# Issuing one stage's stores from GpSimd's queue instead of SyncE's

## The chip, the core and the metric

The kernel runs on one core of one Trainium2 chip. The metric is the device time of one execution in microseconds, as the median of several runs. A profile of one execution goes with it. The engines are named as in the profile: PE (TensorE's matmuls; PEld its weight loads), DVE (VectorE), ACT (ScalarE), POOL (GpSimd) and SP (SyncE). "SPq" is SP's queue of instructions that issue DMAs.

## The reference

The inputs are q, k and v of shape (4, 8, 576, 64) and two pairs of weights, (512, 2048) and (2048, 512). Three stages follow each other:

```python
# attention inside chunks of 64 rows
scores = q_c @ k_c.T / sqrt(64); attn = softmax(scores); out = attn @ v_c
x = out as (2304, 512)
# layer 1: mish
h = x @ w_in;  g = h * tanh(softplus(h));  x = g @ w_out
# layer 2: squareplus
h = x @ w_in2; g = h if h >= 1, 0 if h <= -1, else (h + 1)**2 / 4;  out = g @ w_out2
```

Everything is float32. The kernel reaches that accuracy by splitting each operand into a high and a low part and adding three matmuls for each product (high x high, high x low, low x high).

## The kernel before

**The stages.** The 2304 tokens are cut into 18 tiles of 128. Tiles 0 to 5 go through attention first. Layer 1's first product then has two forms. For the first 768 tokens (two blocks b of 384) it is plain: `up(b, j)` (L672) makes product j of 16 for a block with 12 matmuls (L687) into a bank of PSUM ring "B", 32 products in all. Meanwhile PE runs the attention of tiles 6 to 17 (transposes L558, scores L574, transposes L618, values L630), whose results are the tokens of the second form: `up_seven` (L911), a Strassen-like scheme with seven products (L934) for the other 1536 tokens. The second product of layer 1 is L737, layer 2 is L998 and L811.

**The z buffers.** After `up(b, j)`, ACT applies Mish (L1070) from PSUM into a tile z of the ring "z0", which has three buffers, and one DMA stores the tile to device memory (`spill[j]`, L1073; 192 KB for 384 columns). Much later `g_load` (L715) reads it back for the second product. So a Mish may start only when the store of the Mish three before has landed. ACT takes its instructions in order, so what stands behind the Mish waits too.

**Weights.** `w_part` (L330) loads a block of w_in (L350), decodes it (ACT L358, DVE L365), and splits it: a high part `hi` (L319 on ACT or L321 on DVE) and a low part `lo` (L375), which goes to POOL or DVE. POOL's other work in this stage is the normalisation of attention (L609).

**The order of the work.** `Plan` (L26) keeps a list of all operations with the engine (or the engines to choose from), a planned duration, what they read and write, and a priority. `order()` (L75) simulates the engines with these durations and writes down the order; each engine then runs its instructions in just that order (L1168 to L1184). A DMA is an operation of SP of 0.65 us, then a transfer in a common DMA stream and a lag of 2.2 us until it counts as landed (L141 to L143). All DMAs of this kernel are issued by SP, loads and stores alike, in one planned order. Waits are made from the dependencies; an instruction whose wait is not over holds up all that stand behind it on its engine.

Of the kernel before, what the change touches and what calls it, by code (L numbers as in the profile page):

```python
# [166 lines left out]
def kernel(  # L167
# [20 lines left out]
    nc = tc.nc  # L188
# [97 lines left out]
    def new(name, tag, shape, dtype=F32):  # L286
        size = 4
        for d in shape[1:]:
            size *= d
        at = PLACES[name[0]](*name[1:]) if tag is None else None  # L290
        plan.tile(name, tag, at, size)
        specs[name] = (tag, shape, dtype, size)

    def get(name):
        if name not in T:
            tag, shape, dtype, size = specs[name]
            tile = plan.tiles[name]
            if tag in PSUM:
                t = banks[tag][tile["slot"]]
            elif tag in LENT:  # L300
                at = LENT[tag][2] + tile["slot"] * LENT[tag][1]
                t = area(at, size, F32)
            elif tag is None:
                a, n = WITHIN.get(name[:2], lambda _: (tile["at"], size))(name[-1])
                t = area(a, n)[:, (tile["at"] - a) // 4:(tile["at"] + size - a) // 4]
            else:
                at = base[tag] + tile["slot"] * FIXED[tag][1]
                t = memory[:, at // 4:(at + size) // 4]
                if dtype == U32:
                    t = t.bitcast(dtype)  # L310
            if len(shape) > 2:
                dims = " ".join("abcd"[:len(shape) - 1])
                t = t.rearrange(f"p ({dims}) -> p {dims}", **dict(zip("abcd", shape[1:])))
            T[name] = t
        return T[name]
# [7 lines left out]
    def op(engine, length, emit, **kw):  # L323
        return plan.op(engine, length, emit, **kw)

    def dma(kb, emit, **kw):
        op("SP", 0.65, emit, size=kb * kw.pop("slow", 0.83) / 300.0, **kw)


    def w_part(n, j, tau, release=0.0, after=(), pair=None):  # L330
# [45 lines left out]

        kw = {"prio": tau, "release": release}
        dma(512, load, slow=(1.05, 0.83)[n % 2], reads=after, writes=[raw], tiles=[raw], **kw)
        kw = {"prio": tau}

# [4 lines left out]
        if n == 2:  # L385
            dma(256, lambda _: nc.sync.dma_start(out=wd[j // 2][:, j % 2 * DM:(j % 2 + 1) * DM], in_=get(sh)),
                reads=[sh], writes=[("wd", n, j)], tiles=[sh], prio=tau)
            return
# [6 lines left out]
    def w_load(n, jp, tau, release=0.0, after=()):  # L395
        wf = ("wf", n, jp)
        new(wf, "ld", [P, 2, DM])
        dma(512, lambda _: nc.sync.dma_start(out=get(wf).rearrange("p j f -> p (j f)"), in_=wd[jp]),
            reads=[("wd", n, 2 * jp), ("wd", n, 2 * jp + 1), *after], writes=[wf], tiles=[wf], prio=tau, release=release)
        return wf  # L400
# [271 lines left out]
    def up(b, j, tau):  # L672
        h, w = ("h", 0, b, j), ("w", 0, j)
        new(h, "B", [P, 512])
        start, width = PART(b, j)
        tiles = range(start // P, (start + width) // P)
        x = ("x", OF[tiles[-1]])

        def products(some):
            wt = get(w)  # L680
            xt = get(x).rearrange("p i r k t -> p r k i t")
            xt = xt[:, :, :, tiles[0] - FIRST[x[1]] // P:tiles[-1] + 1 - FIRST[x[1]] // P]
            ps = get(h)[:, 0:width].rearrange("p (i t) -> p i t", t=P)
            for kk in some:
                wh, wl = wt[:, 0, kk * P:(kk + 1) * P], wt[:, 1, kk * P:(kk + 1) * P]
                for y, (a, r) in enumerate(((wh, 0), (wh, 1), (wl, 0))):
                    nc.tensor.matmul(  # L687
                        out=ps, lhsT=a, rhs=xt[:, r, kk],
                        start=(kk == 0 and y == 0), stop=(kk == KD - 1 and y == 2),
                    )  # L690

        n = PIECES if b == 0 and j < EACH else 1
        for k in range(n):
            op("PE", long(width) / n, lambda _, k=k: products(range(k * KD // n, (k + 1) * KD // n)),
               reads=[(x, y, i, c) for y in range(2) for c in range(2) for i in tiles] + [(w, 0), (w, 1)],
               writes=[h], tiles=[h, w, x], prio=tau, late=LATE if n > 1 and k == 0 else 0.0)
        return h, start, width
# [366 lines left out]
    for b in range(len(UP)):  # L1064
        for j in range(NF):
            tau = due(b, j)
            h, start, width = up(b, j, tau)
            z = ("z", 0, b, j)
            new(z, "z0", [P, width])
            op("ACT", 0.17 + width / 1220, lambda _, h=h, z=z, width=width: nc.scalar.activation(  # L1070
                out=get(z), in_=get(h)[:, 0:width], func=AF.Mish
            ), reads=[h], writes=[z], tiles=[h, z], table="mish", prio=tau)
            dma(width / 2, lambda _, z=z, j=j, start=start, width=width: nc.sync.dma_start(  # L1073
                out=spill[j][:, start:start + width], in_=get(z)
            ), reads=[z], writes=[("spill", 0, b, j)], tiles=[z], prio=tau)
    units1 = [(jp, q) for some in (range(NF // 4, NF // 2), range(NF // 4)) for q in (1, 2) for jp in some]
# [138 lines left out]
```

## Time and profile before

| | |
|---|---|
| Time, median of 3 runs | 821.62 us (820.94 to 822.12) |
| Profiled execution, its time | 822.98 us |
| its span, first to last instruction | 821.1 us |
| PE busy in the span | 806.0 us (98%) |
| DVE, ACT, POOL busy | 615.7, 468.7, 43.5 us |
| DMA queues | one for the program's DMAs, 166,736 packets, 212.33 MB |

The profile's page lists the busy time of each engine and the costliest groups of instructions; the trace behind it answers for a stretch, a line or an engine. Times in rows are from the start of the span. In a timeline a row may merge several instructions (xN); what stands in square brackets is the idle time of the engine before the row and what ended it. Matmuls overlap, so rows of PE can overlap by part of a microsecond. The span is 1.9 us shorter than the time of the same execution.

### The profile page before, as it was taken

Reading aid. Unit: us, or ns where it says so; the run is one execution under the profiler, and the core shown is the slowest. Engines: PE = TensorE matmul, PEld = TensorE weight load, DVE = VectorE, ACT = ScalarE, POOL = GpSimd, SP = SyncE. Lnnn points to the kernel's source line nnn. Section 1 sums busy time; section 2 is a strip of 40 time slices with the busy share of each in tenths; the row PEclk is TensorE's granted clock in tenths of the full one; section 3 lists DMA queues with packets and bytes.
Section 4 is the critical chain, followed back from the end, with each engine's and each line's share of the span. In section 5 each row is a group of like instructions: output and inputs, shape, how many; then the busy total and the mean of one; then the engine's idle time right before and its main releaser. Section 6 shows DMA issues by size and latency. Waiting matters only on the chain.

```text
span 821.1 us, 15929 instructions
## 1 busy us (share of the span) xinstructions
PE 806.0 (98%) x6002; PEld 762.7 (93%) x6002; DVE 615.7 (75%) x1092; ACT 468.7 (57%) x733; POOL 43.5 (5%) x39
## 2 busy tenths in 40 slices
PE   8999989999999999999999999999999999999998
PEld 7888979999999988888888899999999999999998
DVE  4876658988888776766777879766777678888883
ACT  4778769756777654545465566655665543333341
POOL 2122111100013000000000000000000000000000
PEclk9999999999999999999999999999999999999999
DMA  9988773479899999899999694796669954444431
GB/s 208 235 247 225 191 178 101 155 249 321 278 367 368 370 386 406 345 395 377 380 407 377 197 345 139 241 367 198 230 254 407 415 184 152 144 139 129 130 103 52
DMA packets 166812, 213.33 MB, mean 260 GB/s; under 512 B 65232, under 2 KB 134352, under 8 KB 163664
## 3 DMA queue, kind: packets, MB, share of 16 engines
q1 hardware_dynamic: 166736, 212.33, 76.3%
q8 instruction: 47, 0.77, 0.4%
q14 instruction: 29, 0.24, 0.1%
HBM read 131.55 MB, written 80.74 MB: 259 GB/s over the span
## 4 chain that ended last, share of the span: by engine, by line
PE 91%; DMA 4%; SPq 2%; DVE 1%; ACT 0%; issue 0%; POOL 0%; ACTq 0%; POOLq 0%; DVEq 0%
PE A L737 13%; PE A L811 11%; PE B L811 11%; PE A L998 11%; PE B L998 11%; PE B L737 11%; PE B L934 9%; PE B L687 5%; PE A L934 4%; DMA memory<-in_moe_w_in_dram 2%; PE A L558 2%; DMA memory<-in_q_dram 1%; SPq L547 1%; PE A L630 1%; PE A L618 1%; PE A L574 1%
## 5 line engine op out<-in xcount | busy, mean ns | idle before, releaser
L319 ACT ACTIVATE r<-memory 128x512 fp32r<-128x512 f32 (+3 forms) x235 | 160.6, 710 | 155.6 <-DVE memory L769 28.2
L737 PE MATMUL A<-r,r 128*128 128x512 f32 (+1 forms) x576 | 114.2, 354 | 0.0
L737 PEld LDWEIGHTS A<-r,r 128*128 128x128 f32 x576 | 95.7, 189 | 14.8
L811 PE MATMUL A<-r,r 128*128 128x256 f32 x768 | 95.9, 283 | 0.0
L811 PEld LDWEIGHTS A<-r,r 128*128 128x128 f32 x768 | 93.9, 192 | 0.0
L811 PE MATMUL B<-r,r 128*128 128x256 f32 x744 | 93.0, 283 | 0.0
L998 PE MATMUL B<-r,r 128*128 128x384 f32 x504 | 92.6, 335 | 0.0
L998 PE MATMUL A<-r,r 128*128 128x384 f32 x504 | 91.1, 334 | 0.0
L811 PEld LDWEIGHTS B<-r,r 128*128 128x128 f32 x744 | 90.9, 192 | 0.0
L737 PE MATMUL B<-r,r 128*128 128x512 f32 x384 | 89.2, 389 | 0.0
L998 PEld LDWEIGHTS B<-r,r 128*128 128x128 f32 x504 | 88.1, 188 | 0.7
L998 PEld LDWEIGHTS A<-r,r 128*128 128x128 f32 x504 | 87.6, 188 | 0.4 <-ACT memory L319 0.3
L737 PEld LDWEIGHTS B<-r,r 128*128 128x128 f32 x384 | 71.9, 188 | 14.8
L783 DVE TENSOR_TENSOR r<-memory,r 128x768 fp32r<-128x768 f32 (+1 forms) x72 | 76.7, 1088 | 11.2 <-ACT r L319 11.1
L934 PE MATMUL B<-r,r 128*128 128x384 f32 x462 | 83.2, 336 | 0.0
L934 PEld LDWEIGHTS B<-r,r 128*128 128x128 f32 x462 | 79.9, 188 | 0.2
L687 PE MATMUL B<-r,r 128*128 128x384 f32 (+2 forms) x384 | 75.6, 345 | 1.5 <-POOL r L375 0.7
L358 ACT ACTIVATE memory<-memory 128x512 f16<-128x512 bf16 x72 | 55.9, 787 | 30.0 <-DMA memory<-in_moe_w_in_dram 15.1
L687 PEld LDWEIGHTS B<-r,r 128*128 128x128 f32 x384 | 65.0, 189 | 4.0 <-POOL r L375 1.2
L720 DVE TENSOR_TENSOR r<-memory,r 128x512 fp32r<-128x512 f32 (+1 forms) x80 | 49.6, 636 | 20.8 <-ACT r L319 20.8
L365 DVE SCALAR_TENSOR_TENSOR memory<-memory 128x512 uint32<-128x512 uint32 x72 | 50.7, 711 | 16.7 <-ACT memory L358 16.6
L769 DVE TENSOR_TENSOR memory<-memory 128x256 f32<-128x256 f32 (+1 forms) x108 | 53.4, 511 | 12.5 <-DMA memory<-z 11.2
(78 smaller groups left out, 954.8 us busy)
## 6 DMA issues: line engine op xcount, KB each, us to landing
memory<-z SPq DMA_DIRECT2D x136, 256.0 KB, 5.2
z<-memory SPq DMA_DIRECT2D x64, 384.0 KB, 4.9
memory<-in_moe_w_in_dram SPq DMA_DIRECT2D x40, 511.0 KB, 5.9
v<-r SPq DMA_DIRECT2D x16, 1024.0 KB, 8.3
memory<-in_moe_w_out_dram SPq DMA_DIRECT2D x32, 511.8 KB, 6.7
v<-r SPq DMA_DIRECT2D x16, 768.0 KB, 7.0
r<-v SPq DMA_DIRECT2D x20, 512.0 KB, 5.5
r<-v SPq DMA_DIRECT2D x8, 1024.0 KB, 10.6
```

The lines of the kernel that those rows point to most:

```text
L319: nc.scalar.activation(out=out, in_=in_, func=AF.Copy)
L358: nc.scalar.activation(out=get(dec).bitcast(F16).rearrange("p (f w) -> p f w", w=2)[:, :, 1], in_=get(raw).rearrange("p f w -> p (f w)").b ...
L365: nc.vector.scalar_tensor_tensor(out=to(sh).bitcast(U32), in0=get(raw)[:, :, 0], scalar=13, in1=get(dec).bitcast(U32), op0=ALU.logical_shi ...
L558: nc.tensor.transpose(out=get(ps)[:, p, :], in_=get(qk)[:, x, 2 * p:2 * p + 2, :].rearrange("t h d -> t (h d)"), identity=ident,)
L687: nc.tensor.matmul(out=ps, lhsT=a, rhs=xt[:, r, kk], start=(kk == 0 and y == 0), stop=(kk == KD - 1 and y == 2),)
L720: op("DVE", 0.15 + width / 930, port=True, emit=lambda _: nc.vector.tensor_tensor(out=get(g)[:, 1], in0=get(zl), in1=get(g)[:, 0].bitcast( ...
L737: nc.tensor.matmul(out=get(y)[:, 0:width], lhsT=l, rhs=r, start=(j == 0 and x == 0), stop=(j == NF - 1 and x == 2))
L769: op("DVE", length, lambda _: nc.vector.tensor_tensor(out=out(), in0=a(), in1=b(), op=ALU.subtract), port=True, reads=reads, writes=writes ...
L783: op("DVE", length, lambda _, a=a, b=b, x=x, c=c: nc.vector.tensor_tensor(out=get(g)[:, :, 1, a:b], in0=get(x)[:, :, c:], in1=get(g)[:, :, ...
L811: nc.tensor.matmul(out=get(ys[bank(x)])[:, half], lhsT=gt[:, l, c], rhs=wt[:, a, r], start=(j == 0 and (half == 0 or end) and y == 0), sto ...
L934: nc.tensor.matmul(out=ps, lhsT=l, rhs=xt[:, r, kk, :], start=(first and kk == 0 and y == 0), stop=(kk == 1 and y == 2), skip_group_check= ...
L998: nc.tensor.matmul(out=ps, lhsT=l, rhs=xt[:, r, kk, :], start=(first and kk == 0 and y == 0), stop=(kk == 1 and y == 2), skip_group_check= ...
```

## The change

The helper `dma` takes an engine and a planned duration, SP and 0.65 us unless something else is given. The store of z after the plain first product of layer 1 gives POOL and 1.1 us, and its DMA is issued with `nc.gpsimd.dma_start`. These are 32 DMAs. Data, sizes, buffers and priorities stay the same; the planner works out a new order for all engines from the new entry.

```diff
     def dma(kb, emit, **kw):
-        op("SP", 0.65, emit, size=kb * kw.pop("slow", 0.83) / 300.0, **kw)
+        at, length = kw.pop("by", ("SP", 0.65))
+        op(at, length, emit, size=kb * kw.pop("slow", 0.83) / 300.0, **kw)
...
-            dma(width / 2, lambda _, z=z, j=j, start=start, width=width: nc.sync.dma_start(
+            dma(width / 2, by=("POOL", 1.1), emit=lambda _, z=z, j=j, start=start, width=width: nc.gpsimd.dma_start(
                 out=spill[j][:, start:start + width], in_=get(z)
             ), reads=[z], writes=[("spill", 0, b, j)], tiles=[z], prio=tau)
```

## Rows read from the trace of the kernel before

**Rows 1.** The profile's page, part 1: busy us of each engine, share of the span.

```profile
PE 806.0 (98%) x6002; PEld 762.7 (93%) x6002; DVE 615.7 (75%) x1092; ACT 468.7 (57%) x733; POOL 43.5 (5%) x39
```

**Rows 2.** Stretches: length; PE, PEld, DVE, ACT, POOL busy us (instructions); clock, DMA share, GB/s.

```profile
30.00:100.00 70.00, 66.57 (x826) 60.42 (x815) 49.48 (x109) 55.27 (x85) 17.35 (x14) 1.00 0.87 227
100.00:110.00 10.00, 6.60 (x119) 5.84 (x118) 5.57 (x11) 3.53 (x7) 0.00 (x0) 0.92 0.86 214
110.00:160.00 50.00, 49.75 (x637) 46.26 (x637) 41.63 (x87) 42.52 (x65) 9.35 (x7) 0.98 0.49 133
160.00:795.00 635.00, 635.00 (x3891) 604.29 (x3890) 489.00 (x822) 348.88 (x548) 11.40 (x8) 1.00 0.79 286
```

**Rows 3.** PE's waits from 30 to 165 us: total, times, longest.

```profile
PE A L574 <- ACT f L319: 3.4, 1, 3.4
...
PE B L687 <- POOL r L375: 0.7, 1, 0.7
```

**Rows 4.** PE's timeline around its longest wait: start, duration, instructions.

```profile
102.72 2.36 PE L687 MATMUL B<-r,r 128*128 128x384 f32 x12
108.48 1.40 PE L574 MATMUL A<-memory 64*64 64x64 f32 x32 [3.40 <-ACT f L319]
109.81 1.97 PE L558 MATMUL A<-ident,memory 128*128 128x128 f32 x8
...
113.85 0.69 PE L574 MATMUL A<-memory 64*64 64x64 f32 x32
114.47 1.09 PE L558 MATMUL A<-ident,memory 128*128 128x128 f32 x8
```

**Rows 5.** ACT's timeline over the same wait.

```profile
96.30 0.49 ACT L1070 ACTIVATE memory<-B 128x384 f32<-128x384 f32 x1 [1.53 <-DMA z<-memory]
...
100.06 0.66 ACT L319 ACTIVATE memory<-A 128x512 f32<-128x512 f32 x1
107.12 1.03 ACT L1070 ACTIVATE memory<-B 128x384 f32<-128x384 f32 x2 [6.40 <-DMA z<-memory]
108.05 0.66 ACT L319 ACTIVATE f<-A 128x256 f32<-128x256 f32 x2
```

**Rows 6.** SP's timeline of DMA issues before it.

```profile
95.78 2.65 SPq L547 DMA_DIRECT2D memory<-in_v_dram  x4
...
101.12 0.78 SPq L539 DMA_DIRECT2D memory<-in_k_dram  x1
102.00 2.13 SPq L1073 DMA_DIRECT2D z<-memory  x3
```

**Rows 7.** Line L1073, the stores: issue ns (min/median/max), who waited, landing.

```profile
L1073 SPq DMA_DIRECT2D z<-memory x32: 319/544/2877, 35.8 to 146.1; - x32
...
  ACT memory L1070: 10.2, 4
...
DMA to landing us min/median/max: 1.9/3.6/6.3
```

**Rows 8.** POOL's groups from 30 to 150 us, then lines L609 and L375.

```profile
L609 POOL TENSOR_TENSOR memory<-memory,ri 128x512 f32<-128x512 f32 x12 | 14.6, 1217 | 59.5 <-DVE ri L603 24.7 <-ACT memory L319 16.6 <-ACT memory L595 9.5
L375 POOL TENSOR_TENSOR r<-memory,r 128x512 fp32r<-128x512 f32 x8 | 10.3, 1284 | 37.0 <-ACT r L319 25.5 <-DVE r L321 11.5
...
L609 POOL TENSOR_TENSOR memory<-memory,ri x13: 1042/1045/1860, 32.2 to 152.8; 128x512 f32<-128x512 f32 x13
...
L375 DVE TENSOR_TENSOR r<-memory,r x13: 683/685/1685, 35.7 to 272.6; 128x512 fp32r<-128x512 f32 x13
...
  PEld B L687: 1.2, 2
```

**Rows 9.** POOL's timeline: second L375 of the stage, L609 after the stall.

```profile
45.14 1.30 POOL L375 TENSOR_TENSOR r<-memory,r 128x512 fp32r<-128x512 f32 x1 [11.89 <-ACT r L319]
...
112.44 1.04 POOL L609 TENSOR_TENSOR memory<-memory,ri 128x512 f32<-128x512 f32 x1 [16.61 <-ACT memory L319]
```

**Rows 10.** DVE's commonest copy from SBUF to SBUF, 30 to 150 us: count, busy, mean ns.

```profile
L321 DVE CAST r<-memory 128x512 fp32r<-128x512 f32 x5 | 2.1, 423 | 0.1
```

## Prediction

> **What bounds the kernel now.** I read the page's first two parts, then a table of stretches, then who made TensorE (PE) wait, then the timelines around the one long wait. The page says that PE is busy 98% of an 821.1 us span [rows 1], so only the places where it is not busy can give time back. The table of stretches shows where those are [rows 2]: from 160 to 795 us PE is busy 635.00 of 635.00 us; from 30 to 160 us, the stage in which layer 1's plain products run beside the attention of the later rows, it idles 3.43 us (30 to 100), 3.40 us (100 to 110) and 0.25 us (110 to 160), 7.1 us in all. That stage is also the only one in which the moved stores are issued (35.8 to 146.1 us, [rows 7]).
>
> Half of the 7.1 us is one wait. PE's list of waits has one entry of 3.4 us, on ACT's copy, and one of 0.7 us on POOL [rows 3]. The timeline of PE shows it: twelve matmuls of L687 begin at 102.72 and take 2.36 us, then nothing until 108.48 [rows 4]. ACT's timeline says why: it does its last work at 100.06 + 0.66 = 100.72, idles 6.40 us for the landing of a z store, does two Mish at 107.12, and only then the copy that PE is waiting for, at 108.05 [rows 5]. Mish writes into a ring of three z buffers, so it waits for the store three before it. That store's Mish ended at 96.30 + 0.49 = 96.79, but SyncE (SP) issued it at 102.00, because SP was issuing four v loads (95.78) and four q and k loads up to 101.90 in the order that it was given [rows 6]. It landed 5.1 us later. So 5.2 us of the delay is SP's queue and 5.1 us is the transfer.
>
> The cost of this place is more than the idle time. The granted clock is 0.92 in the stretch of the wait and 0.98 in the one after it, 1.00 before and long after [rows 2]: for a while after the idle, 1.2 GHz and not 2.4. The same work done then and shortly after differs [rows 4]: L574 x32 took 1.40 against 0.69 and L558 x8 1.97 against 1.09. That is 0.71 + 0.88 = 1.59 us. Wait and clock together: 3.40 + 1.59 = 5.0 us.
>
> **The change part by part.** *Removed from SP:* 32 issues with a median of 0.544 us [rows 7], 17.4 us of a queue that issues nearly without a break around the stall [rows 6]. Loads behind them can be issued that much sooner. PE's waits on ACT and POOL are the ones that show, not loads, so I count this as nothing; what the loads wait for otherwise is free buffers.
>
> *The store's way to the memory:* on POOL it is queued behind normalisations (L609) and low halves of weights (L375) only. POOL idles 16.61 us before its L609 at 112.44 [rows 9], from 95.83 on, so the store of the Mish that ended at 96.79 is issued at once. What such an issue costs POOL the trace does not show, for POOL issues no DMA. From below: the shortest SP issue of these stores, 0.32 us; from above, the longest, 2.88 us [rows 7]. POOL's own fixed-size work lies between: 1.05 us for L609, 1.28 us for L375 [rows 8]. I take 1.05, of POOL's rows the one nearest to SP's median. Landing: 1.9 to 6.3 us after issue, median 3.6 [rows 7]; I take 5.1 again, as the 16 DMA engines stay as loaded (share 0.86, [rows 2]). Landing at 96.79 + 1.05 + 5.1 = 102.9 instead of 107.1. ACT then does its two Mish (1.03 us) and the copy (at most 0.66) by 104.6, and PE finishes L687 at 105.08: the wait is gone and with it the slow clock. Worth 5.0 us; with the 6.3 us landing the copy ends at 105.8 and 0.7 us of the wait stays, too short to matter.
>
> The other three waits of ACT for these stores add 10.2 - 6.4 = 3.8 us [rows 7] and go too, but none of PE's longer waits follows from them: nothing counted.
>
> *Added to POOL:* 32 x 1.05 = 33.6 us. POOL is busy 14.6 + 10.3 = 24.9 us between 30 and 150 us [rows 8], so 58.5 of 120 us are used; it has room. But it is in order, and a store waits in it for its Mish. Behind it stand L609, then PE's transposes (L618), and L375, then PE's L687. Of the two it is L375 that has the less cover: PE waited 0.7 us for it once [rows 3], its weight loads 1.2 us in two waits [rows 8]. I charge one store in front of one such low half, 1.05 us. The bounds are 0 and the slower rival (b) below.
>
> *The list order:* the planner's cost for the store goes from 0.65 on SP to 1.1 on POOL, and everything after is placed anew. L375 may go to POOL or DVE; with POOL fuller some go to DVE, 0.685 us each [rows 8]. All eight would be 5.5 us more on a DVE that is busy 49.48 of 70 us [rows 2]. I count nothing, and keep the range wide for it: the 635 us without a gap show what a new order can lose.
>
> *Sum:* the profiled run took 822.98 us (span 821.1). 822.98 - 5.0 + 1.05 = 819.0 us. The median of the runs, 821.62, is 1.36 below that run: **817.7 us**.
>
> *A rule that speaks against it.* POOL's own work shows what happens when it is held up: L609 takes 1.045 us mostly and 1.860 at worst [rows 8]. At 1.86 us for every store, 32 x 1.86 + 24.9 = 84.4 us still fit into 120. The Trainium skill ("SBUF — State Buffer", section "SBUF: two separate sides") says that a DMA issued by GpSimd has its descriptors written through SBUF ports that it shares with VectorE, and is locked out while VectorE runs a copy from SBUF to SBUF in a two-port mode; it gives about 620 ns alone and about 3100 ns overlapped. DVE copies of that kind between 30 and 150 us are mainly 5 of 423 ns, 2.1 us [rows 10], so by the rule as worded hardly a store is touched. No row of this trace shows a DMA issued by POOL, so none can bear it out. If every store met the longer time, 32 x 3.1 + 24.9 = 124 us would not fit into 120, and the estimate by this page would be a loss of some 4 us in place of the gain.
>
> **The rivals.**
> (a) *DVE takes over.* The PE work after 110 us comes 5 us sooner, but DVE does not, and PE waits for it further on. For: DVE is busy 41.63 of 50 us in 110 to 160, ACT 42.52. Against: DVE idles 4.43 of the 10 us of the stall, since it is held by the same chain, so its work moves forward with PE's. Time: the 5.0 us come back as another wait, 821.6, no change.
> (b) *Slower: low halves stand behind stores.* Of the eight L375 of POOL in 30 to 150 us, all but the first come at 45 us or later, where the weights arrive late (POOL idles 37.0 us before them, waiting for the high halves, [rows 8]; the second is at 45.14, [rows 9]), and in 30 to 100 PE idles 3.43 us. If each of the seven has a store in front that waits for its Mish or takes 1.28 us, and PE has no cover: 7 x 1.28 = 9.0 us, less 5.0: 821.62 + 4.0 = 825.6. It decides from 5.0 / 7 = 0.71 us per low half. For: the planner may put a store there. Against: stores become ready when PE finishes a product, low halves two or three products ahead, and DVE may take them.
> (c) *POOL is held at each issue by what DVE does* (DVE is busy seven tenths of the stage, [rows 2]) until it is full. With the upper bound of 2.88 us for each store, 32 x 2.88 + 24.9 = 117.1 of 120 us. Then a store goes out as late as it did on SP, the stall stays, and the two low halves that PE's loads waited for come 2.88 us later each: 821.62 + 5.8 = 827.4. Against: POOL's longest held row is 0.82 us over its usual one [rows 8]. The page of the Trainium skill named above has a price that is this high.
> (d) *More goes than I count:* SP's shorter queue also ends the small waits of 30 to 100 us: 7.1 us of idle and 1.6 us of clock, 8.7 in all: 812.9.
> The change does what it says in any case: the 32 issues leave SP.
>
> **How the numbers follow.** Forecast (817.7, its own range 815 to 819.9) 0.46; (a) 0.18; (b) 0.22; (c) 0.06; (d) 0.08. A measurement of this kernel tells about 0.2%, 1.6 us, from no change. Faster: forecast and (d), 0.54. Same: (a), 0.18. Slower: (b) and (c), 0.28. The range goes down past (d), since its 8.7 us could be joined by a better order, to 811.5, and up past (b) to 826.0, which leaves (c) out.
>
> **What will show it.** Right: no issue of L1073's successor on SP; ACT's wait for z stores falls from 10.2 us to under 3; PE's 3.4 us wait on ACT's copy is gone and the granted clock stays 1.00 between 100 and 120 us; PE busy in 30 to 160 us at the same work, that stage some 4 us shorter and the rest as long as before. The price of POOL's issue is read from its rows: about 1 us for the sum, 2 or more for (c). For (a), PE waits for DVE between 110 and 165 us instead. For (b), PE's wait for POOL's L375 grows from 0.7 us to several. Wrong in another way: PE idle in 160 to 795 us, where there is none; then the new order and not the queue decided.

## The result, and the profile after

The changed kernel takes 814.12 us (median of 4 runs, 813.21 to 816.41) beside 821.87 us for the kernel before (4 runs). The ratio is 0.9908 with a 95% interval of 0.9883 to 0.9933, so 7.8 us faster. A second measurement gave 814.29 beside 822.52 us, ratio 0.9898 (0.9864 to 0.9932). The profiled execution took 813.21 us, its span is 811.4 us. The prediction was 817.7 us, with a range from 811.5 to 826.0; the forecast's own range, 815 to 819.9, was missed by 0.9 us.

The page of the changed kernel shows PE busy for less time and a larger share, and a second DMA queue, which holds the moved stores: 6.29 MB.

```profile
PE 804.2 (99%) x6002; PEld 761.7 (94%) x6002; DVE 614.4 (76%) x1092; ACT 469.5 (58%) x732; POOL 59.6 (7%) x72
...
q1 hardware_dynamic: 162128, 206.03, 74.8%
q0 software_dynamic: 2048, 6.29, 2.2%
```

The table of stretches, to be read against [rows 2] (its first line here, the first 30 us, has no partner there; before it had 25.58 us of PE):

```profile
0.00:30.00 30.00, 27.75 (x418) 25.66 (x418) 19.44 (x47) 14.77 (x26) 6.71 (x11) 1.00 0.98 215
30.00:100.00 70.00, 68.53 (x845) 62.73 (x837) 48.98 (x108) 59.38 (x90) 28.59 (x36) 1.00 0.98 255
100.00:110.00 10.00, 10.00 (x123) 9.33 (x123) 9.50 (x20) 8.65 (x14) 3.19 (x4) 1.00 0.63 159
110.00:160.00 50.00, 50.00 (x608) 46.91 (x607) 44.41 (x86) 40.62 (x66) 10.18 (x13) 1.00 0.44 133
160.00:795.00 635.00, 634.80 (x3914) 604.18 (x3913) 487.99 (x828) 345.26 (x538) 10.93 (x8) 1.00 0.79 284
```

This splits the 9.7 us between the two spans. PE's idle time shrinks by 2.2 us in the first 30 us, by 2.0 from 30 to 100, by 3.4 from 100 to 110, by 0.25 from 110 to 160, grows by 0.2 from 160 to 795 and shrinks by 0.3 after that. PE's busy time shrinks by 1.8 us (806.0 to 804.2) with the granted clock at 1.00 from 30 to 160 us, where it was 0.92 and 0.98 in two stretches [rows 2]. The 2.2 us of the first 30 us are not the change's: there every engine runs the same instructions in the same order in both, up to the first store. Without them the profiles differ by 7.5 us, which is what the medians say.

PE's waits from 30 to 165 us (total, times, longest); the 3.4 us of [rows 3] are gone, and the wait for POOL's low halves (L376 is L375 of before, as all lines from here on are one higher) is the same 0.7 us:

```profile
PE B L688 <- POOL r L376: 0.7, 1, 0.7
PE A L559 <- DVE memory L589: 0.4, 1, 0.4
PE B L688 <- ACT r L319: 0.3, 1, 0.3
```

The line of the store (the partner of [rows 7]): what POOL's issue costs, what POOL waited for ahead of it, who waited for the store, and how long it took to land.

```profile
L1074 POOL DMA_DIRECT2D z<-memory x32: 539/554/712, 33.2 to 133.9; - x32
...
  ACT memory L1071: 38.1, 22
...
  ACT memory L1071: 1.0, 2
DMA to landing us min/median/max: 2.1/3.6/6.0
```

An issue on POOL takes 0.554 us in the median, as on SP (0.544). But SP's reach up to 2.88 us and add up to 24.9 us, POOL's stay within 0.71 and add up to 18.0. ACT waits 1.0 us for stores in place of 10.2. Landing is unchanged, with a median of 3.6 us from the start of the issue. What changed is the time from the end of a Mish to the issue: a mean of 3.42 us (9.37 at worst) before, 0.43 (1.78) after, worked out from the 32 pairs of each trace. The 38.1 us are the other side of it: POOL stands idle that long, in 22 waits, for Mish to end; PE's wait for POOL's low halves did not grow by it. In the kernel before, SP's list of waits from 30 to 160 us begins so:

```profile
SPq L1073 <- ACT memory L1070: 12.2, 10, 3.8
```

This row says more than is there: it counts a Mish that ends while an issue is running, also where it isn't the one that the store needs. With each store set beside its own Mish, SP stood idle at stores in four places, 6.5 us in all: 0.2 us at 53.9 us, and 0.3, 2.1 and 3.8 us at 116.7, 119.2 and 145.7 us, behind the stall. Ahead of the stall SP was not standing at stores but issuing: the 17 stores before 102.00 us held it for 17.1 us, five of them for 1.4 to 2.9 us each. Why some issues are that long the trace doesn't say.

### The profile page after: what moved, and what is told of

Read it like the earlier page. It is cut to its first block, busy times and chain, and to the rows that moved or that the text cites. A ratio compares the mean times of both kernels' runs of the same rounds, so it can differ in the third digit from the quotient of the medians.

```text
span 811.4 us, 15954 instructions
## 1 busy us (share of the span) xinstructions
PE 804.2 (99%) x6002; PEld 761.7 (94%) x6002; DVE 614.4 (76%) x1092; ACT 469.5 (58%) x732; POOL 59.6 (7%) x72
## 3 DMA queue, kind: packets, MB, share of 16 engines
q0 software_dynamic: 2048, 6.29, 2.2%
## 4 chain that ended last, share of the span: by engine, by line
PE 95%; DMA 2%; SPq 1%; DVE 1%; ACT 0%; issue 0%; POOL 0%; DVEq 0%; ACTq 0%
PE A L738 14%; PE A L812 11%; PE B L812 11%; PE B L738 11%; PE B L999 11%; PE A L999 10%; PE B L935 10%; PE B L688 7%; PE A L935 4%; PE A L559 2%; PE A L631 1%; PE A L575 1%; PE A L619 1%; DMA memory<-in_moe_w_in_dram 1%; DMA r<-v 1%; SPq L548 1%
## 5 line engine op out<-in xcount | busy, mean ns | idle before, releaser
L319 ACT ACTIVATE r<-memory 128x512 fp32r<-128x512 f32 (+3 forms) x229 | 157.3, 712 | 156.0 <-PE A L738 30.4
L721 DVE TENSOR_TENSOR r<-memory,r 128x512 fp32r<-128x512 f32 (+1 forms) x80 | 49.8, 634 | 25.5 <-ACT r L319 25.2
```

Of the source, the lines that this page charges most:

```text
L319: nc.scalar.activation(out=out, in_=in_, func=AF.Copy)
L721: op("DVE", 0.15 + width / 930, port=True, emit=lambda _: nc.vector.tensor_tensor(out=get(g)[:, 1], in0=get(zl), in1=get(g)[:, 0].bitcast( ...
```

## The experiments

Six kernels take the change apart, two look for the cost of POOL's queue, one repeats the changed kernel, and one moves other DMAs. Ratios are to the kernel before on the same chip.

| Kernel | Time, us | Before, us | Ratio (95%) |
|---|---|---|---|
| queue alone | 815.87 | 822.30 | 0.9934 (0.9912 to 0.9956) |
| order alone | 818.87 | 822.30 | 0.9969 (0.9950 to 0.9987) |
| SP, stores first | 817.77 | 822.30 | 0.9951 (0.9932 to 0.9970) |
| cost 0.55 | 818.28 | 822.30 | 0.9958 (0.9934 to 0.9982) |
| three moved | 819.53 | 822.52 | 0.9951 (0.9930 to 0.9972) |
| three left | 814.76 | 822.52 | 0.9905 (0.9873 to 0.9938) |
| changed kernel again | 814.29 | 822.52 | 0.9898 (0.9864 to 0.9932) |
| POOL kept busy | 816.56 | 822.52 | 0.9931 (0.9905 to 0.9958) |
| v loads moved | 814.91 | 820.63 | 0.9932 (0.9907 to 0.9958) |

**Queue alone.**

```diff
-            dma(width / 2, by=("POOL", 1.1), emit=lambda ...: nc.gpsimd.dma_start(
+            dma(width / 2, by=("SP", 0.65), emit=lambda ...: nc.gpsimd.dma_start(
```

> The stores are issued by POOL, but the planner still counts them on SP, so PE, DVE and ACT keep the order of the kernel before, instruction by instruction, and SP keeps its order without the 32 stores. If the queue is what counts (the store no longer stands behind SP's loads): ACT's 6.4 us wait and PE's 3.4 us wait go, and at least 5.0 of the 7.7 us come: 816.9 us or less. If the planner's new order of all engines is what counts: 821.6 us, no change.

It takes 815.87 us, 6.4 less than before by the medians, 5.4 by the ratio. The order of PE, DVE and ACT is that of before to the instruction, so this gain is the queue's. ACT's waits for z stores from 30 to 160 us fall to 0.5 us, and PE is busy 10.00 of 10 us where the stall was:

```profile
100.00:110.00 10.00, 10.00 (x134) 9.26 (x127) 8.44 (x20) 8.07 (x13) 3.69 (x5) 1.00 0.81 182
```

**Order alone.** The other half: the planner has its new entry, SP issues.

```diff
-            dma(width / 2, by=("POOL", 1.1), emit=lambda ...: nc.gpsimd.dma_start(
+            dma(width / 2, by=("POOL", 1.1), emit=lambda ...: nc.sync.dma_start(
```

> The planner counts the stores on POOL at 1.1 us, as in the changed kernel, but SP issues them, at the place in time that the planner gave them for POOL. PE, DVE and ACT have the order of the changed kernel. If the order of all engines is what counts: 814 us. If the queue is what counts: SP's own list is again in the way, ACT waits for z stores again for 6 us or more, 819 to 823 us. If it is only the store's place in SP's list (now nearer to its Mish, since the planner sees SP free): 815 to 817 us with SP as the issuer.

It takes 818.87 us, 3.4 less than the median before. The long stall does not come back in this order, but other waits come, among them one of 1.5 us for which the profile names no releaser, and PE loses 3.3 us from 30 to 100. ACT waits for stores again, and the mean time from Mish to issue is 2.51 us:

```profile
ACT memory L1071 <- DMA z<-memory: 3.7, 4, 1.6
```

So the new order by itself gives about 3 us of what the whole change gives, and the queue by itself 5.4 to 6.4; they don't add up, since the same stall is in both. Between queue alone (0.9934) and the whole change (0.9908 and 0.9898) the intervals overlap.

**SP, stores first.** The stores stay on SP at 0.65 us, with priority -50:

```diff
-            ), reads=[z], writes=[("spill", 0, b, j)], tiles=[z], prio=tau)
+            ), reads=[z], writes=[("spill", 0, b, j)], tiles=[z], prio=-50.0)
```

> SP issues the stores and is counted at 0.65 us, but a store that is ready goes ahead of every load in the planner's choice (priority -50 instead of the product's due time). If only the place in SP's list counts: the delay from Mish to issue falls from a mean of 3.5 us to about 1, ACT's 6.4 us wait goes, 815 to 817 us. If SP's issue time is what counts (17.4 us of a queue that issues without a break): loads come later instead, and no more than half is gained, 818 us or more.

It takes 817.77 us, 4.5 less. The delay from Mish to issue fell only to a mean of 2.07 us, with SP still making all the issues, and one wait of 3.9 us on ACT is left. The priority also gave all engines a new order, so how much of the 4.5 us is the store's place in SP's list is not shown.

**Cost 0.55.** The changed kernel with the planner's cost for POOL at what the trace shows:

```diff
-            dma(width / 2, by=("POOL", 1.1), emit=...
+            dma(width / 2, by=("POOL", 0.55), emit=...
```

> The changed kernel with the planner's cost of the store on POOL at 0.55 us, what the trace shows for such an issue, instead of 1.1. Queue: the stores go out as in the changed kernel, 814.1 us within 0.3%. Order: another list for every engine, so the time may move by more than 2 us either way.

It takes 818.28 us, about 4 us more than the changed kernel. The stores go out as promptly (0.48 us after their Mish). What it loses, it loses in two places: PE idles 1.2 us more from 30 to 100 us (2.64 us against 1.47), and 2.8 us more from 160 to 795 us, in waits that the changed kernel does not have. PE's waits from 110 us on:

```profile
PE A L935 <- ACT f L319: 1.6, 1, 1.6
PE B L738 <- DVE r L721: 1.0, 1, 1.0
PE A L738 <- DVE r L721: 0.4, 1, 0.4
```

Here order decides: a truer entry in the planner gave the worse list.

**Three moved, and three left.** In the order of before, only the three stores that SP issued at 102.00 us [rows 6] go to POOL; then all but those three.

```diff
+            dma(width / 2, emit=lambda _, ..., at=(nc.gpsimd if (b, j) in ((0, 15), (1, 2), (1, 3)) else nc.sync): at.dma_start(
...
+            dma(width / 2, emit=lambda _, ..., at=(nc.gpsimd if (b, j) not in ((0, 15), (1, 2), (1, 3)) else nc.sync): at.dma_start(
```

> The kernel before, with all engines in its order; only the three stores that SP issued at 102.00 us (blocks and products (0,15), (1,2), (1,3)) are issued by POOL, the other 29 stay on SP. If the stall is local, as the prediction priced it: ACT's 6.4 us and PE's 3.4 us wait go, the clock stays up, 5.0 us come: about 817 us beside 822. If a store that is late elsewhere takes its place: less than 2 us.

> The complement: the kernel before in its order, 29 stores on POOL, the same three on SP behind its loads. If the stall is these three stores' place behind eight loads: it stays, and only the small waits of 30 to 100 us go, 1 to 2 us: 820 to 821. If what counts is how many issues SP has to make, so that with 26 fewer before them the loads go out early and the three stores with them: the stall goes too, 816 to 817.

Three moved: 819.53 us, 3.0 less by the medians and 4.0 by the ratio. The stall is gone (PE busy 10.00 of 10 us from 100 to 110), but part of it is given back: PE idles 4.42 us from 30 to 100, where it idled 3.43 before, and it waits once in layer 1's second product. PE's waits from 165 us on are this one, where before had none:

```profile
PE B L738 <- DVE r L721: 1.7, 1, 1.7
```

Why is not shown: in three left, in the same order, PE comes to this product earlier (251.87 us against 254.53) and does not wait.

Three left: 814.76 us, as fast as the whole change, with the three late stores still on SP and still behind its loads in the list. SP's timeline says how. It has got so far ahead that it comes to the three in time; they go out 0.39, 0.03 and 0.07 us after their Mish:

```profile
91.63 0.87 SPq L540 DMA_DIRECT2D memory<-in_k_dram  x1
92.59 2.43 SPq L1074 DMA_DIRECT2D z<-memory  x3
95.88 6.33 SPq L548 DMA_DIRECT2D memory<-in_v_dram  x8
```

This is against the theory of the prediction, that the three stores' place behind eight loads is the cause. The place was the symptom. The cause is that SP as a whole had fallen some five us behind by then.

**The v loads moved.** That theory has a test without any z store on POOL: give POOL 24 of the 48 v loads of tiles 6 to 17.

```diff
-                    nc.sync.dma_start(
+                    (nc.gpsimd if i >= 6 and c == 0 else nc.sync).dma_start(
                         out=get(vt)[(r ^ c) * CH:((r ^ c) + 1) * CH, c], in_=v[b, r::2, s:s + CH, :].rearrange("h p d -> p h d")
```

> The kernel before in its order with all z stores on SP; instead 24 of the 48 v loads of tiles 6 to 17 are issued by POOL (15.6 us of SP's issue time, about as much as the 17.4 us of the stores). If SP's backlog is the cause, whoever makes it: the stores go out within about 1 us of their Mish, the stall at 105 us goes and some 5 us come, unless POOL, which now waits in order for free v buffers, holds up its normalisations. If the stores gain because they have a queue of their own: ACT's 6.4 us wait stays, 821 to 823 us.

It takes 814.91 us beside 820.63: ratio 0.9932, the same as queue alone. All z stores are on SP, in the old order, and the 6.4 us wait is gone; three waits of 2.8 us in all are left. The stores do not go out within about 1 us of their Mish, as I expected, but after a mean of 2.55 us (3.42 before).

```profile
ACT memory L1071 <- DMA z<-memory: 2.8, 3, 1.8
```

So the gain does not need the stores to have a queue of their own. Fewer issues on SP are enough, z stores or v loads alike. One thing stays together in these runs: what left SP always went to POOL's queue, so a part that a second queue has as such isn't separated from the shorter list. With all issues on SP (SP, stores first) 4.5 us came, in a new order.

**POOL kept busy.** Five fills of a small buffer behind each store, in the changed kernel:

```diff
+            ), [nc.gpsimd.memset(scratch, 0.0) for _ in range(5)]), reads=[z], ...
```

> The changed kernel with five idle fills of a small buffer on POOL behind each store, about 1 us, 32 us of POOL in all; the order is unchanged. They stand in front of the normalisations and the low halves of weights, as the charge of the prediction and its slower rival had it for the store itself. If POOL has cover: less than 1.6 us more than the changed kernel. If each low half behind a store delays PE (rival b): 7 x 1 us, 5 to 7 us more.

It takes 816.56 us, 2.3 more than the changed kernel beside it; the intervals overlap. PE's waits from 30 to 165 us now name POOL (L620 is L618, L689 is L687 of before):

```profile
PE A L620 <- POOL memory L611: 1.5, 3, 0.7
PE B L689 <- POOL r L377: 1.0, 2, 0.6
```

Waiting behind POOL exists, more for the normalisations (1.5 us, 0.2 before) than for the low halves of the slower rival (1.0 us, 0.7 before). At 1 us more on each store it costs about 2 us and not 7, and the store's own 0.55 us costs PE nothing that shows.

**Copies on DVE beside the issue.** Six copies of 128 columns from z to a small buffer on DVE for each store.

```diff
+            ... ([nc.vector.tensor_copy(scratch, get(z)[:, 0:128]) for _ in range(6)], nc.gpsimd.dma_start(
```

> The changed kernel with six short copies from SBUF to SBUF on DVE for each store, which become ready with the store (192 copies of 128 columns, about 25 us of DVE). It asks what an issue on POOL costs beside such copies. If POOL is locked out while DVE runs them, as the prediction's rule had it: the issue's median rises from 0.55 us to 1 us or more and to 3 us at worst, as the stores of the first 35 us (0.71 us) hint. If not: it stays at 0.54 to 0.60 us. The time rises by some us for DVE's sake in either case.

It took 847.14 us in its one run. DVE's 192 copies, 52.5 us of busy time, are the likely reason, which is not shown. The issue on POOL did not change:

```profile
L1075 DVE COPY scratch<-memory x192: 175/227/1628, 33.4 to 167.1; 128x128 f32<-128x128 f32 x192
L1075 POOL DMA_DIRECT2D z<-memory x32: 539/557/710, 33.7 to 159.7; - x32
```

In 26 of the 32 issues a copy ran at the same time, in most for over 0.4 us of the 0.55. Only the first issue is longer (0.71 us), in both kernels; so that hint of mine was the first issue's, not DVE's.

**The changed kernel again.**

> The changed kernel once more, on the same chip as the runs beside it: 0.991 of the kernel before, about 7.5 us. If the first 30 us of the profile of before were late by chance (its order is the same up to the first store), PE reaches its 450th matmul at 34 to 36 us here as in the other kernels, and the rest of the difference lies between 60 and 120 us.

814.29 us. In this profile PE idles 4.34 us in the first 30 us, as in that of before (4.42) and not as in the first of the changed kernel (2.25). The start of a run varies by about two us with the same instructions. PE reaches its 450th matmul at 36.3 us, not by 36 us as expected (36.8 before, 35.0 in the first of the changed kernel). And the half of the expectation that put all the rest between 60 and 120 us holds only roughly: some 5 us lie around the old stall.

## Why the prediction was right, point by point

*The direction, the place and the mechanism were right.* The wait of ACT for a late z store, PE's 3.4 us behind it and the slow clock after it went, and that stretch gave what it was priced at. Forecast 5.0; measured 3.4 us of idle and 1.8 us less of busy time, 5.2.

*The sum was too small by 3.6 us*, 817.7 against 814.1, and the terms that were mis-sized are these.

The charge of 1.05 us for a store in front of a low half: measured as nothing. The issue is 0.554 us and not 1.05, and PE's wait for POOL's low halves is 0.7 us in both profiles, although a low half begins right behind a store three times (at 42.30, 51.74 and 58.59 us). I had taken POOL's data instructions as the nearest rows; SP's own issue was the nearer one.

"Loads behind them can be issued that much sooner", which I counted "as nothing", and "nothing counted" for ACT's other three waits: here the step failed. PE's idle time from 30 to 100 us fell from 3.43 to 1.47 us, 2.0 us. I looked only at who made PE wait, and no load stood there. But SP's backlog reaches PE through the loads of the weights. SP's timeline of before shows one store's issue of 2.88 us, and behind it, without a break, loads of v and of w_in:

```profile
57.14 2.88 SPq L1073 DMA_DIRECT2D z<-memory  x1
60.11 2.01 SPq L547 DMA_DIRECT2D memory<-in_v_dram  x2
62.21 0.56 SPq L350 DMA_DIRECT2D memory<-in_moe_w_in_dram  x1
62.81 1.26 SPq L547 DMA_DIRECT2D memory<-in_v_dram  x2
64.17 0.55 SPq L350 DMA_DIRECT2D memory<-in_moe_w_in_dram  x1
```

For the last of these ACT idles 2.50 us, and what stands behind it on ACT and DVE makes PE wait twice, 1.5 us in all:

```profile
70.13 0.79 ACT L358 ACTIVATE memory<-memory 128x512 f16<-128x512 bf16 x1 [2.50 <-DMA memory<-in_moe_w_in_dram]
```

```profile
71.78 0.69 PE L630 MATMUL A<-memory 64*64 64x64 f32 x32 [0.60 <-ACT memory L319]
73.36 1.09 PE L558 MATMUL A<-ident,memory 128*128 128x128 f32 x8 [0.88 <-DVE memory L588]
```

In the changed kernel the same load, the 15th of w_in, goes out 5.8 us sooner, and PE has no wait from 59.7 to 80 us:

```profile
58.35 0.55 SPq L351 DMA_DIRECT2D memory<-in_moe_w_in_dram  x1
```

The other profiles sort the same way. In the seven profiles in which 24 or more issues had left SP (the one with DVE's copies not counted), this load goes out at 58.4 to 61.6 us and PE idles 1.3 to 2.7 us from 30 to 100. In the four in which at most three had left it, it goes out at 63.1 to 64.7 us and PE idles 3.3 to 4.4 us. That was rival (d), to which I gave 0.08. With 812.9 it was nearer than the forecast. This term and the charge make 3.1 of the 3.6 us; the rest is not assigned.

The cause as I put it, a store behind eight given loads, was one step short: "because SP was issuing four v loads (95.78) and four q and k loads up to 101.90 in the order that it was given". With the same place in the list, and the other 29 stores gone from the queue, the store is punctual (three left); with 24 fewer v loads the three go out 2.0 to 2.8 us after their Mish, where it was 4.6 to 5.2. The rows that would have told me are the issues themselves: I priced all 32 at the median, 17.4 us, where their sum is 24.9 us, and 17.1 of it lies ahead of the stall.

*The profiled run of before* was also slow by chance in its first 30 us. I had set its 1.36 us over the median aside in the sum, which was right.

*Rival (a), DVE takes over,* did not come in this stage, but later and smaller: in four of the kernels that keep less of the gain (three moved, cost 0.55, and 0.6 us in queue alone and in order alone) PE waits for DVE's L721 in the second product, 0.6 to 1.7 us. In the changed kernel it does not. *Rival (b)* stayed small: PE's wait for low halves is 0.7 us, and 1.0 us with POOL kept busy. *Rival (c)* fell: no issue on POOL took more than 0.71 us in the first profile of the changed kernel, and none more than 1.04 us in any. What the Trainium skill ("SBUF — State Buffer", section "SBUF: two separate sides") says of descriptors starved by DVE's copies is not borne out here, by 26 issues that overlapped with short copies; long copies were not tried. *The list order* I left in the range, and that is where it belongs: with the stores on POOL and prompt, three lists gave 814, 816 and 818 us.

What stays open is how much of the 7.8 us the new list adds to the queue's 5.4 to 6.4, as the intervals of the two overlap, and what part a second queue has as such.

## What to carry to other kernels

When a wait ends with a DMA's landing, split it at the issue: here half of it was a queue that issued in order and had fallen behind, and that half was bought back by giving 24 to 32 of that queue's DMAs, of one kind or another, to an idle engine's queue. Count the issuing queue's time by the sum of its issues and not by the median, and follow a late load from its issue to what the busiest engine waits for: the engine named in the wait may itself have waited for it. And where a planner orders everything, run a change once in the old order: it separates what the change does from what a new list does, which here was as much as 4 us.

## What was not expected of the hardware

An issue on POOL costs POOL 0.54 to 0.58 us, the first of a run 0.71 to 0.99 (and single ones 0.77 and 1.04 in two of the kernels), and lands in a median of 3.6 us from its start as one on SP does, for 192 KB in rows of 1.5 KB; issues of 64 KB v loads in rows of 256 bytes took 0.616 us on POOL beside 0.607 on SP. DVE, busy 49 of 70 us beside it in the changed kernel, did not lengthen it.

```profile
L548 SPq DMA_DIRECT2D memory<-in_v_dram x48: 595/607/1785, 2.7 to 142.0; - x48
...
L548 POOL DMA_DIRECT2D memory<-in_v_dram x24: 615/616/777, 44.5 to 142.2; - x24
```

A wait of PE of 3.4 us was followed by 1.2 GHz for 3.4 us (from 108.3 us on); PE's busy time is 1.8 us less in the changed kernel, where the wait is gone and the clock stayed at 2.4 GHz through the stage.
